# A windowed attention with channel mixing on one core: two-token rows, halves of v moved by DMA, x transposed by the crossbar

## The chip, the cores and the metric

The kernel runs on one core of a Trainium2 chip. The metric is the device time in microseconds of one execution, as the median of several runs. A core has five engines with their own instruction streams: TensorE (PE; its weight loads are listed as PEld), VectorE (DVE), ScalarE (ACT), GpSimd (POOL) and SyncE (SP), which here issues nearly all the transfers. The engines wait for each other by semaphores.

## What is computed

Inputs are q, k and v of shape [4, 8, 768, 64] (4 sequences, 8 heads, 768 tokens, 64 wide), all float32. Attention is causal with a window of 128 tokens, and the first four tokens (the sinks) are seen by every query:

```python
scores = q @ k.T / sqrt(64)
keep = (pos_k < 4) | ((pos_q - pos_k >= 0) & (pos_q - pos_k < 128))
a = softmax(where(keep, scores, -1e9))
x = (a @ v)                        # heads side by side: [4, 768, 512]

x_prev = x shifted by one token, 0 ahead of the first
xk = mu_k * x + (1 - mu_k) * x_prev
xr = mu_r * x + (1 - mu_r) * x_prev
k = relu(xk @ w_k)                 # [.., 1024]
v = (k * k) @ w_v                  # [.., 512]
out = sigmoid(xr @ w_r) * v
```

(The reference writes the first `k` and `v` of the second half with names of their own; they have nothing to do with the attention's.)

## The kernel before

The kernel works in 12 blocks of 256 tokens, u = 0 to 11, three for each sequence: b is the sequence and T = 0, 1, 2 the block in it. Every operation is registered with an engine, and a list for each engine (ORDER) gives the order of the operations by number; another (CHOICE) gives the engine of those that could run on more than one. Buffers come from pools and are handed out in that order.

A block goes through four steps. `prepare` casts k and q to bf16 and transposes them, so that the head dimension lies on partitions, with TensorE and an evacuation, or with a transposing DMA through the crossbar (k from block 4 on, q from block 8 on). Where TensorE transposes, k and q come with two neighbouring tokens in one row (`j` is the parity), and the evacuation undoes that by a strided write. v comes with one token in a row and 256 B in a run:

```python
# load
if name == "v":
    for g in range(2):
        s0 = 256 * T + 128 * g
        ... nc.sync.dma_start(out=buf[key][:, g, :, :],
                              in_=v[b, :, s0:s0 + 128, :].rearrange("h p d -> p h d"))
...
# otherwise, two tokens in a row
        ... nc.sync.dma_start(out=buf[key][:, h0:h1, :, :].rearrange("p h j d -> p h (j d)"),
                in_=src[b, h0:h1, 256 * T:256 * T + 256, :].rearrange(
                    "h (p j) d -> p h (j d)", j=2))
...
# prepare: evacuation of transposed k and q
out=buf[key][:, 2 * half:2 * half + 2, :, :].rearrange("p c g (t j) -> p c j (g t)", j=2),
in_=buf[psk].bitcast(BF16)[:, 0:512].rearrange("p (c j t) -> p c j t", c=2, j=2)
```

`attend` works by pairs of heads (c = 0 to 3). Scores of two pairs are made in one go, the exponential follows on ScalarE, VectorE multiplies it by a mask of ones and zeros, and TensorE multiplies by v. A column of ones beside v gives the sum of the weights; VectorE divides. In a first block (T = 0) no earlier keys exist and the scores are 768 wide for a pair instead of 1024. For later blocks the sinks are scored apart (`es`, `vsink`).

```python
jobs = [(kt[:, c, 0, :], 128, 384, qt[:, c, :, :]), (kt[:, c, 1, :], 384, 512, qt[:, c, 1, :])]
if T > 0:
    jobs.append((buf["kt", u - 1][:, c, 1, :], 0, 128, qt[:, c, 0, :]))
for (lhs, o0, o1, rhs) in jobs:
    for a in range(2):
        rows = slice(64 * a, 64 * a + 64)
        nc.tensor.matmul(out=sc[:, a, o0:o1], lhsT=lhs[rows], rhs=rhs[rows], ...)
...
nc.scalar.activation(out=buf[ek][:, :, lo:], in_=buf[sck][:, :, lo:], func=AF.Exp, scale=scale)
...
nc.vector.tensor_tensor(out=at, in0=at, in1=m, op=ALU.mult)      # the mask
...
# values: for each half g of the queries, the sinks, then two key blocks for each head
```

`mix` transposes x with TensorE, copies it from PSUM into `xt` (a sequence's tokens side by side, with a zero ahead), and blends neighbouring tokens:

```python
P.op("PE", 225.0, transpose, ...)            # 4 transposes for each half of the channels
P.op("ACT", act(512), evacuate(...), ...)    # or VectorE; two for each block
...
nc.vector.tensor_tensor(out=buf[tk], in0=xt[:, c0:c0 + 2, t0:t0 + 256],
                        in1=xt[:, c0:c0 + 2, t0 - 1:t0 + 255], op=ALU.subtract)
# then for xk and xr, and for each of four channel groups
nc.vector.scalar_tensor_tensor(out=buf[key][:, c0 + i, :], in0=buf[tk][:, i, :],
    scalar=mu[w][:, c0 + i:c0 + i + 1], in1=xt[:, c0 + i, t0 - 1:t0 + 255],
    op0=ALU.mult, op1=ALU.add)
```

`ffn` then makes keys (32 matmuls of 256 columns), relu, square, the gate (8 matmuls of 512, a tanh in place of the sigmoid) and the product with w_v (16 matmuls of 512), and stores 128 tokens at a time. The step of block u-1 is interleaved with the attention of block u. While TensorE has nothing to do early on, it multiplies a tile `warm` by itself.

Of the kernel before, what the change touches and what calls it, by code (L numbers as in the profile page):

```python
# [16 lines left out]

CHOICE = {
    78: "ACT", 81: "ACT", 82: "ACT", 84: "ACT", 86: "ACT", 88: "DVE", 93: "DVE", 94: "DVE", 96:
    "DVE", 100: "DVE", 101: "DVE", 127: "DVE", 133: "DVE", 135: "DVE", 136: "DVE", 139: "ACT",  # L20
    140: "DVE", 149: "DVE", 190: "DVE", 191: "ACT", 192: "ACT", 217: "DVE", 264: "DVE", 272:
    "DVE", 277: "DVE", 304: "DVE", 342: "DVE", 345: "DVE", 347: "DVE", 351: "ACT", 353: "DVE",
    360: "DVE", 422: "DVE", 428: "ACT", 429: "ACT", 498: "DVE", 500: "DVE", 503: "DVE", 506:
    "DVE", 507: "ACT", 519: "DVE", 585: "ACT", 586: "ACT", 653: "DVE", 657: "DVE", 659: "DVE",
    662: "DVE", 671: "DVE", 735: "DVE", 737: "ACT", 738: "DVE", 743: "DVE", 750: "DVE", 814:
    "DVE", 815: "ACT", 824: "DVE", 884: "DVE", 886: "DVE", 890: "ACT", 891: "ACT", 1002: "DVE",
# [3 lines left out]
QD = range(8, 12)  # L30

XD = ()

BEGIN = {"SP": 800.0, "PE": 1260.0, "ACT": 2600.0, "DVE": 930.0, "POOL": 930.0}

TOGETHER = 2

RING = 2600
# [10 lines left out]
        89, 92, 105, 95, 98, 103, 116, 108, 113, 131, 137, 141, 128, 124, 119, 155, 134, 157,  # L49
        148, 183, 189, 168, 235, 207, 208, 211, 212, 219, 220, 160, 165, 171, 176, 215, 193,  # L50
        180, 200, 216, 186, 237, 290, 298, 291, 294, 299, 302, 248, 303, 225, 295, 240, 245,
        306, 223, 227, 276, 231, 228, 251, 260, 232, 266, 256, 310, 263, 283, 269, 311, 318,
        343, 308, 314, 329, 315, 348, 366, 374, 367, 375, 321, 370, 394, 326, 371, 332, 337,
        396, 274, 352, 378, 359, 379, 382, 407, 384, 386, 421, 387, 444, 452, 445, 453, 399,
        426, 404, 474, 410, 415, 390, 430, 391, 456, 437, 457, 448, 472, 485, 449, 462, 525,
        529, 526, 530, 499, 537, 460, 504, 538, 468, 509, 469, 553, 477, 482, 533, 493, 488,
        534, 511, 564, 556, 464, 578, 465, 541, 518, 543, 561, 549, 583, 572, 550, 587, 545,
        567, 631, 601, 546, 602, 605, 613, 606, 594, 629, 642, 614, 619, 609, 617, 610, 639,
        634, 677, 681, 678, 682, 663, 645, 689, 705, 707, 685, 650, 686, 690, 625, 670, 718,
        710, 621, 626, 693, 622, 760, 756, 764, 757, 761, 765, 721, 695, 740, 726, 715, 774,  # L60
        784, 701, 749, 768, 742, 769, 795, 702, 787, 792, 697, 772, 698, 816, 776, 780, 777,
        781, 834, 830, 838, 831, 835, 798, 839, 858, 860, 842, 803, 846, 843, 823, 854, 848,
        868, 863, 871, 855, 906, 914, 907, 850, 915, 851, 879, 874, 910, 892, 911, 918, 899,
        919, 934, 936, 922, 924, 930, 947, 931, 972, 939, 973, 980, 944, 981, 950, 976, 958,
        977, 955, 984, 926, 965, 985, 927, 990, 988, 1000, 1008, 1004, 1001, 1012, 1005, 1013,
        1009, 992, 1020, 996, 993, 997, 1016, 1018, 1021, 1028, 1024, 1029, 1025,
    ),
    "DVE": (
        70, 71, 88, 93, 94, 100, 96, 107, 101, 112, 109, 114, 110, 136, 104, 115, 118, 127, 123,
        143, 125, 120, 133, 121, 126, 135, 149, 144, 150, 151, 145, 152, 190, 146, 159, 147,  # L70
        164, 79, 80, 153, 69, 170, 140, 175, 161, 162, 166, 172, 167, 177, 173, 178, 154, 195,
        196, 202, 197, 204, 203, 210, 217, 198, 222, 205, 206, 83, 239, 244, 304, 199, 85, 241,
        305, 242, 246, 214, 247, 255, 218, 87, 277, 250, 293, 297, 278, 229, 252, 301, 253, 233,
        257, 258, 279, 264, 342, 285, 347, 280, 281, 286, 288, 345, 320, 287, 312, 325, 316,
        272, 336, 289, 322, 331, 323, 327, 282, 328, 333, 338, 334, 339, 369, 353, 275, 373,
        354, 360, 357, 361, 381, 355, 377, 363, 356, 362, 422, 388, 398, 403, 409, 400, 414,
        405, 401, 365, 411, 416, 406, 417, 412, 358, 364, 447, 432, 392, 433, 439, 434, 441,
        440, 455, 459, 498, 481, 476, 503, 451, 528, 500, 487, 506, 435, 492, 510, 436, 470,
        478, 479, 483, 443, 484, 494, 555, 495, 489, 540, 490, 442, 536, 557, 571, 513, 558,
        560, 532, 466, 514, 519, 562, 520, 563, 516, 566, 573, 521, 574, 515, 522, 589, 551,  # L80
        568, 590, 569, 517, 524, 547, 523, 653, 633, 592, 638, 596, 659, 598, 657, 591, 597,
        604, 644, 635, 640, 636, 641, 649, 599, 616, 600, 612, 665, 646, 593, 608, 647, 651,
        709, 652, 668, 662, 666, 692, 667, 711, 671, 672, 674, 673, 675, 712, 627, 680, 623,
        669, 735, 720, 714, 725, 722, 723, 676, 684, 727, 728, 688, 759, 716, 741, 717, 763,
        791, 786, 750, 767, 738, 743, 788, 789, 793, 744, 703, 794, 745, 771, 751, 747, 802,
        746, 753, 752, 754, 699, 818, 778, 782, 797, 819, 748, 821, 833, 799, 755, 800, 837,
        804, 805, 814, 862, 841, 867, 824, 825, 820, 845, 826, 864, 827, 865, 869, 884, 856,
        822, 878, 886, 870, 828, 873, 852, 875, 880, 881, 876, 909, 829, 917, 894, 897, 913,
        901, 895, 921, 902, 938, 903, 943, 896, 932, 949, 940, 941, 945, 946, 951, 954, 952,
        904, 956, 957, 898, 960, 961, 905, 967, 975, 962, 969, 968, 928, 979, 963, 971, 987,  # L90
        983, 1002, 964, 1003, 1007, 970, 1011, 1015, 994, 998, 1022, 1030, 1026,
    ),
    "ACT": (
        91, 90, 97, 111, 106, 99, 68, 67, 117, 130, 122, 132, 142, 138, 129, 182, 188, 163, 158,
        184, 78, 156, 174, 169, 81, 139, 209, 221, 236, 213, 179, 185, 194, 201, 181, 191, 187,
        243, 238, 292, 82, 300, 192, 254, 226, 249, 84, 296, 307, 86, 224, 259, 265, 261, 262,
        268, 267, 284, 270, 340, 324, 319, 344, 309, 335, 330, 349, 368, 376, 395, 372, 418,
        402, 397, 380, 420, 383, 423, 408, 385, 413, 351, 425, 446, 454, 427, 480, 475, 431,
        496, 438, 428, 501, 458, 450, 473, 486, 463, 527, 531, 429, 491, 461, 505, 539, 559,
        554, 507, 577, 535, 512, 570, 575, 579, 580, 582, 542, 544, 565, 584, 585, 588, 637,  # L100
        632, 603, 586, 655, 595, 607, 615, 630, 620, 643, 618, 611, 648, 679, 683, 664, 706,
        708, 713, 687, 691, 731, 729, 719, 733, 694, 724, 737, 758, 766, 762, 696, 775, 790,
        785, 770, 808, 796, 806, 801, 773, 812, 810, 817, 832, 836, 840, 859, 861, 866, 844,
        847, 815, 882, 849, 877, 872, 888, 908, 916, 893, 912, 900, 935, 920, 937, 942, 890,
        923, 891, 925, 948, 974, 953, 982, 959, 966, 986, 978, 991, 989, 1006, 1014, 1010, 1019,
        1017,
    ),
    "POOL": (
        73, 72, 74, 75, 76, 102, 77, 273, 271, 350, 508, 661, 739,
    ),  # L110
    "SP": (
        0, 1, 2, 3, 4, 5, 7, 6, 16, 8, 9, 10, 11, 15, 17, 12, 18, 13, 14, 19, 20, 25, 23, 24,
        21, 234, 22, 341, 346, 28, 30, 29, 313, 26, 27, 419, 424, 31, 230, 33, 34, 35, 32, 497,
        36, 317, 502, 37, 40, 38, 389, 39, 45, 393, 41, 576, 581, 42, 467, 43, 44, 46, 47, 654,
        656, 660, 658, 548, 48, 51, 49, 50, 471, 53, 52, 732, 730, 734, 736, 54, 628, 57, 58,
        55, 552, 56, 624, 809, 807, 704, 813, 811, 59, 60, 61, 779, 63, 64, 62, 700, 883, 885,
        889, 887, 65, 857, 66, 853, 933, 929, 783, 995, 999, 1023, 1031, 1027,
    ),
}


class Plan:

# [8 lines left out]
    def pool(self, name, tiles):  # L137
        self.pools[name] = list(tiles)

    def op(self, engine, cost, emit, rank, reads=(), writes=(), take=(), hold=(), port=False,  # L140
           lag=None, service=0.0, descs=128, mode=0, alts=None):
        i = len(self.ops)
        if i in CHOICE:
            engine = CHOICE[i]
# [5 lines left out]
    def schedule(self):  # L150
# [42 lines left out]
        while any(lines.values()):  # L193
# [32 lines left out]
            if o["port"]:  # L226
                port[o["engine"]] = t + o["cost"]
# [53 lines left out]
def kernel(  # L281
# [36 lines left out]
    for name in ("ks", "qs", "vs"):  # L318
        pool(name, 3, [128, 2, H, D] if name == "vs" else [128, H, 2, D], FP32)
# [640 lines left out]
```

The softmax here doesn't subtract the row's maximum and nothing guards it: scores larger than these inputs give would overflow.

## Time and profile before

| | before |
|---|---|
| median of 3 runs | 171.7 us (170.59 to 172.16) |
| span of the profiled execution | 169.6 us |
| VectorE instructions, GpSimd instructions | 403, 31 |
| transfers: mean rate, packets | 199 GB/s, 82803 |
| HBM read, written | 24.12 MB, 6.29 MB |
| transposes through the crossbar | 16 of k, 8 of q; median 2.5 and 2.4 us from issue to landing |
| loads of v | 24 of 256 KB; median 4.6 us to landing |

The profile page gives for each engine the time in which an instruction was in work. Instructions of an engine overlap at their ends, so that the mean duration of one in a group is more than the distance from its start to the next start. Where the pace matters it is read from the list of instructions in order of time, whose columns are start, duration, engine, line of the kernel, operation and operands; consecutive ones of a kind are merged and counted (x12). In the slices, each of 40 figures stands for 4.24 us, in tenths. A group line ends with the idle time of the engine just before its instructions and with what ended most of it.

### The profile page before, as it was taken

What the parts mean: (1) busy time and instruction counts of PE and PEld (TensorE: products, weight loads), DVE (VectorE), ACT (ScalarE), POOL (GpSimd) and SP (SyncE); (2) the same over time, 40 slices, a digit from 0 to 9 for tenths busy, and PEclk for the clock granted to TensorE, in tenths of its full rate; (3) what the DMA queues carried; (4) which work ended last, traced back from release to release, by engine and by line L of the source; (5) the groups of instructions that cost most, each with busy time, mean ns of one, the idle gap of its engine ahead of it and who ended that gap; (6) DMA issues with size and microseconds to landing.
All of it is one profiled execution on the core that took longest, in us unless ns stands there. A gap on an engine that the chain in (4) does not pass through costs nothing.

```text
span 169.6 us, 4184 instructions
## 1 busy us (share of the span) xinstructions
PE 160.0 (94%) x1602; PEld 105.7 (62%) x1602; DVE 153.4 (90%) x403; ACT 129.0 (76%) x208; POOL 13.5 (8%) x31
## 2 busy tenths in 40 slices
PE   7977879799999999999999999999999999999992
PEld 2544658664657667767567786756476775877551
DVE  6288898999999999999999999999999999799542
ACT  3588797999898999897979986866829849953320
POOL 6330000000200010050000200030000000000000
PEclk9995699999999999999999999999999999999999
DMA  5999989999938979999579489969969858103033
GB/s 142 238 275 320 344 192 326 356 335 276 191 86 214 254 172 231 184 263 287 135 183 221 97 207 225 181 168 233 252 147 266 195 109 233 62 4 124 2 124 124
DMA packets 82803, 33.82 MB, mean 199 GB/s; under 512 B 64736, under 2 KB 77280, under 8 KB 82784
## 3 DMA queue, kind: packets, MB, share of 16 engines
q1 hardware_dynamic: 81728, 33.56, 80.0%
q8 instruction: 12, 0.20, 0.5%
q10 hardware_dynamic: 1056, 0.00, 0.4%
q14 instruction: 7, 0.06, 0.1%
HBM read 24.12 MB, written 6.29 MB: 179 GB/s over the span
## 4 chain that ended last, share of the span: by engine, by line
PE 82%; DVE 10%; DMA 3%; SPq 1%; issue 1%; ACT 0%; POOL 0%; DVEq 0%
PE bank L888 24%; PE bank L839 23%; PE bank L870 12%; PE bank L713 7%; PE sc L654 6%; DMA vs<-in_v_dram 3%; PE bank L752 3%; PE bank L569 2%; PE bank L701 2%; DVE e L690 2%; DVE xk L789 2%; SPq L387 1%; DVE x L729 1%; PE bank L631 1%; PE bank L809 1%
## 5 line engine op out<-in xcount | busy, mean ns | idle before, releaser
L839 PE MATMUL bank<-xk,wk_sb 128*128 128x256 bf16 x384 | 50.5, 273 | 1.1 <-DVE wk_sb L513 0.9
L676 ACT ACTIVATE e<-sc 128x1024 bf16<-128x1024 f32 (+1 forms) x48 | 44.6, 966 | 4.4 <-PE sc L654 4.4
L888 PE MATMUL bank<-wv_h,kk 128*128 128x512 bf16 x184 | 45.8, 379 | 0.0
L839 PEld LDWEIGHTS <-wk_sb 128*128 128x128 bf16 x384 | 35.3, 98 | 9.3 <-DVE wk_sb L513 1.4
L849 ACT ACTIVATE rl<-bank 128x512 bf16<-128x512 f32 x45 | 26.2, 607 | 10.3 <-PE bank L839 7.8
L690 DVE TENSOR_TENSOR e<-e,mask 128x1024 bf16<-128x1024 bf16 (+1 forms) x48 | 30.1, 639 | 0.4 <-POOL ksink L608 0.3
L888 PEld LDWEIGHTS <-kk 128*128 128x128 bf16 x184 | 16.7, 98 | 15.7 <-issue 0.5
L870 PE MATMUL bank<-wr_sb,xr 128*128 128x512 bf16 x96 | 24.2, 379 | 0.0
L789 DVE SCALAR_TENSOR_TENSOR xk<-td,mu,xt 128x256 bf16<-128x256 bf16 x48 | 22.4, 493 | 0.1
L789 DVE SCALAR_TENSOR_TENSOR xr<-td,mu,xt 128x256 bf16<-128x256 bf16 x48 | 22.5, 477 | 0.0
L876 ACT ACTIVATE th<-bank 128x512 f32<-128x512 f32 x24 | 14.8, 620 | 7.8 <-PE bank L870 7.7
L729 DVE TENSOR_TENSOR x<-bank,rec 128x256 bf16<-128x256 f32 x48 | 19.4, 416 | 0.6 <-DVE rec L726 0.3
L897 DVE SCALAR_TENSOR_TENSOR ob<-th,bank 128x512 f32<-128x512 f32 x23 | 15.6, 681 | 4.7 <-ACT th L876 2.6
L861 DVE TENSOR_TENSOR kk<-rl 128x512 bf16<-128x512 bf16 x48 | 19.4, 416 | 0.1
L713 PE MATMUL bank<-vb,e 128*128 128x65 bf16 x352 | 19.2, 195 | 0.2
L713 PEld LDWEIGHTS <-e 128*128 128x128 bf16 x352 | 16.7, 99 | 3.1 <-issue 0.6
L654 PE MATMUL sc<-qt,kt 64*128 64x128 bf16 (+1 forms) x256 | 14.8, 247 | 1.1 <-ACT kt L577 0.7
L870 PEld LDWEIGHTS <-xr 128*128 128x128 bf16 x96 | 8.9, 98 | 8.6 <-issue 0.3
L654 PEld LDWEIGHTS <-kt 64*128 64x128 bf16 x256 | 9.5, 97 | 7.3 <-issue 4.0
L761 ACT COPY xt<-bank 128x512 bf16<-128x512 bf16 x15 | 8.8, 587 | 5.3 <-PE bank L752 4.5
L701 PE MATMUL bank<-vsink,es 128*128 128x130 bf16 x64 | 12.4, 220 | 0.3 <-ACT rl L849 0.3
L779 DVE TENSOR_TENSOR td<-xt 128x512 bf16<-128x512 bf16 x24 | 10.5, 440 | 0.1
(63 smaller groups left out, 163.9 us busy)
## 6 DMA issues: line engine op xcount, KB each, us to landing
vs<-in_v_dram SPq DMA_DIRECT2D x24, 256.0 KB, 4.6
out_dram<-ob SPq DMA_DIRECT2D x23, 256.0 KB, 3.3
ks<-in_k_dram SPq DMA_DIRECT2D x18, 256.0 KB, 4.8
qs<-in_q_dram SPq DMA_DIRECT2D x7, 512.0 KB, 7.3
qs<-in_q_dram SPq DMA_DIRECT2D x10, 256.0 KB, 5.3
w<-in_moe_w_k_dram SPq DMA_DIRECT2D x2, 1024.0 KB, 10.3
w<-in_moe_w_v_dram SPq DMA_DIRECT2D x2, 1024.0 KB, 10.0
ks<-in_k_dram SPq DMA_DIRECT2D x3, 512.0 KB, 8.2
```

Of the source, the lines that this page charges most:

```text
L654: nc.tensor.matmul(out=sc[:, a, o0:o1], lhsT=lhs[rows], rhs=rhs[rows], start=True, stop=True)
L676: nc.scalar.activation(out=buf[ek][:, :, lo:], in_=buf[sck][:, :, lo:], func=AF.Exp, scale=scale)
L690: nc.vector.tensor_tensor(out=at, in0=at, in1=m, op=ALU.mult)
L701: nc.tensor.matmul(out=o[:, g, :, :], lhsT=buf["es", u][:, 128 * g:128 * g + 128], rhs=vsink[b % 2][:, 2 * c:2 * c + 2, :], start=True, st ...
L713: nc.tensor.matmul(out=o[:, g, a, :], lhsT=e[:, a, e0:e0 + 128], rhs=rhs, start=(T == 0 and i == 0), stop=(i == len(blocks) - 1), skip_gro ...
L729: P.op("DVE", dve(256), lambda ok=ok, rk=rk, c=c: nc.vector.tensor_tensor(out=buf["x", u][:, :, 128 * c:128 * c + 128].rearrange("p g (a d ...
L789: nc.vector.scalar_tensor_tensor(out=buf[key][:, c0 + i, :], in0=buf[tk][:, i, :], scalar=mu[w][:, c0 + i:c0 + i + 1], in1=xt[:, c0 + i, t ...
L839: nc.tensor.matmul(out=ps[:, i, :], lhsT=wk_sb[:, c, 128 * f:128 * f + 128], rhs=xk[:, c, :], start=(c == 0), stop=(c == NC - 1), skip_gro ...
L849: nc.scalar.activation(out=buf[rk], in_=buf[psk].rearrange("p (i t) -> p i t", i=2), func=AF.Relu)
L861: P.op("DVE", dve(512, 0.52), lambda f2=f2, rk=rk: nc.vector.tensor_tensor(out=buf["kk", u][:, 2 * f2:2 * f2 + 2, :], in0=buf[rk], in1=buf ...
L870: nc.tensor.matmul(out=buf[psk], lhsT=buf["xr", u][:, c, 128 * g:128 * g + 128], rhs=wr_sb[:, c, :], start=(c == 0), stop=(c == NC - 1))
L888: nc.tensor.matmul(out=buf[psk], rhs=wv_h[:, f, :], lhsT=buf["kk", u][:, f, 128 * g:128 * g + 128], start=(f == 0), stop=(f == NF - 1))
```

## The change

The arrangement of tokens changes. All of q, k and v now come with two neighbouring tokens in a row (512 B in a run), and the parities are kept apart from there on: a block of 256 queries is two groups of 64 pairs of tokens, ordered odd before even, keys of a whole sequence lie in one tile, even before odd, and stores take every second row of the output. So the strided evacuation of k and q goes, and with it the one-token loads of v, k and q.

- A group's window then begins in the middle of a block's rows. The value matmul of the first group needs half of the rows of the block before and half of its own in one tile `vj`; these halves are moved by DMA within the chip for blocks from 3 on, and by a copy on VectorE or ScalarE before that.
- In the first blocks of sequences 2 to 4 (u = 3, 6, 9) the first 64 pairs see only themselves; both parities of their 64 keys are stacked over the 128 partitions, so that one matmul does for two.
- Blocks 0 and 1 get no mask on VectorE: TensorE writes a bias (0 or -30000) into the scores' PSUM first, by a matmul with the identity, and the scores are added.
- x of blocks 6 to 11 is transposed by the crossbar and not by TensorE.
- The fused blend (difference times mu plus neighbour) becomes three kinds of step: a difference of 512 elements, a scaling by mu (on VectorE or ScalarE), and an addition of 512 elements. An edge copy, on GpSimd or VectorE, puts the last token of a group beside the first of the next.
- mu comes as rows and is transposed on TensorE. GpSimd may take casts of k, q and a weight. CHOICE, ORDER and the constants that the lists were made with are new throughout, and the early loads come in halves by heads, with two blocks of q, k and v ahead of w_k.

```diff
+BIAS = (0,1)
+XD = range(6,12)
+VJD = range(3, 12)
+STACK = (3, 6, 9)
...
-            if name == "v":
-                for g in range(2):
-                    ... in_=v[b, :, s0:s0 + 128, :].rearrange("h p d -> p h d")
+            key, src = (name, u), {"k": k, "q": q, "v": v}[name]
+            ... in_=src[b, h0:h1, 256 * T:256 * T + 256, :].rearrange("h (p j) d -> p h (j d)", j=2)
...
-                    out=buf[key][:, 2 * half:2 * half + 2, :, :].rearrange(
-                        "p c g (t j) -> p c j (g t)", j=2),
+                    out=buf[key][:, 2 * half:2 * half + 2, :, :],
...
+            for g, w in ((1, u - 1), (0, u)):
+                if u in VJD:
+                    P.op("SP", 400.0, lambda g=g, w=w: nc.sync.dma_start(
+                        out=buf[vj][64 - 64 * g:128 - 64 * g].rearrange("p j h d -> p (j h d)"),
+                        in_=buf["vb", w][64 * g:64 * g + 64].rearrange("p j h d -> p (j h d)")), rank,
...
+            for j in range(2):
+                for g in range(2):
+                    at = 128 * T + 64 * (g - 1) * (T > 0)
+                    for a in range(2):
+                        rows = slice(64 * a, 64 * a + 64)
+                        nc.tensor.matmul(
+                            out=sc[:, a, :].rearrange("p (j g t) -> p j g t", j=2, g=2)[:, j, g],
+                            lhsT=kt[rows, c, j, at:at + 128], rhs=q2[rows, g],
+                            start=u not in BIAS, stop=True, skip_group_check=u in BIAS)
+        def biased(cs):
+            for c in cs:
+                for a in range(2):
+                    nc.tensor.matmul(out=buf["sc", u, c][:, a, :], lhsT=ident, start=True,
+                                     rhs=bias[T].to_broadcast([128, 2, 2, 128]), stop=False,
+                                     skip_group_check=True)
...
+            else:
+                P.op("SP", 1200.0, lambda g=half: nc.sync.dma_start_transpose(
+                    out=xt[:, :, at + g, 16:144], in_=buf["x", u][:, g, :]),
...
+            return lambda: copy(out=xt[:, :, at + 1:at + 1 + n, 15:16],
+                                in_=xt[:, :, at:at + n, 79:80])
...
-            P.op("DVE", dve(512, 0.5), lambda c0=c0, tk=tk: nc.vector.tensor_tensor(
-                out=buf[tk], in0=xt[:, c0:c0 + 2, t0:t0 + 256],
-                in1=xt[:, c0:c0 + 2, t0 - 1:t0 + 255], op=ALU.subtract), ...
-                        nc.vector.scalar_tensor_tensor(
-                            out=buf[key][:, c0 + i, :], in0=buf[tk][:, i, :],
-                            scalar=mu[w][:, c0 + i:c0 + i + 1],
-                            in1=xt[:, c0 + i, t0 - 1:t0 + 255], op0=ALU.mult, op1=ALU.add)
+            P.op("DVE", dve(512, 0.52), lambda g=g: nc.vector.tensor_tensor(
+                out=block(xr, g), in1=behind(g), op=ALU.subtract, ...
+                    nc.vector.tensor_scalar(
+                        out=buf[key][:, c, :], in0=buf[xr][:, c, :],
+                        scalar1=mu[w][:, c:c + 1], scalar2=None, op0=ALU.mult)
+                    # or, on ScalarE
+                    nc.scalar.activation(out=buf[key][:, c, :], in_=buf[xr][:, c, :],
+                                         func=AF.Copy, scale=mu[w][:, c:c + 1])
+                    nc.vector.tensor_tensor(out=part, in0=part, in1=behind(g), op=ALU.add)
...
-                nc.sync.dma_start(out=out[b, s0:s0 + 128, :], in_=buf[bk])
+                nc.sync.dma_start(out=out[b, s0 + 1 - g:s0 + 256:2, :], in_=buf[bk])
```

The lists ORDER and CHOICE, the building of masks and sinks, and the model's constants are cut here.

## The prediction

> **What bounds the kernel now.** I read the spans and clocks first (one core, 169.6 us in the profile, clock 0.98), then the busy shares and the slices, then windows of 5 us, then TensorE in order of time, and last the costliest groups and the DMA part. From the page:
>
> ```profile
> PE 160.0 (94%) x1602; PEld 105.7 (62%) x1602; DVE 153.4 (90%) x403; ACT 129.0 (76%) x208; POOL 13.5 (8%) x31
> ...
> PE   7977879799999999999999999999999999999992
> ...
> DVE  6288898999999999999999999999999999799542
> ...
>
> ```
>
> TensorE is full from about slice 9 on, and so nearly is VectorE. Before that both have holes, and the clock falls to half. The windows say it more exactly (columns: stretch, its length, then busy time and instructions of TensorE, weight loads, VectorE, ScalarE, GpSimd, the clock, the DMA share and GB/s):
>
> ```profile
> 10.00:15.00 5.00, 3.29 (x41) 2.06 (x41) 4.68 (x13) 4.02 (x7) 1.34 (x3) 0.83 1.11 264
> 15.00:20.00 5.00, 4.64 (x53) 3.28 (x52) 3.73 (x12) 3.92 (x7) 0.00 (x0) 0.50 1.05 378
> 20.00:25.00 5.00, 3.24 (x29) 2.16 (x26) 5.00 (x12) 5.00 (x8) 0.00 (x0) 0.98 0.89 199
> ...
> 30.00:35.00 5.00, 4.12 (x50) 3.21 (x50) 5.00 (x13) 5.00 (x8) 0.00 (x0) 1.00 1.05 367
> 35.00:40.00 5.00, 5.00 (x44) 2.97 (x43) 5.00 (x14) 5.00 (x9) 0.00 (x0) 1.00 1.16 310
> ```
>
> A busy TensorE need not be at its peak, so I take its pace from starts in order of time:
>
> ```profile
> 154.11 3.66 PE L839 MATMUL bank<-xk,wk_sb 128*128 128x256 bf16 x32
> 157.60 4.48 PE L888 MATMUL bank<-wv_h,kk 128*128 128x512 bf16 x20
> 161.92 1.89 PE L870 MATMUL bank<-wr_sb,xr 128*128 128x512 bf16 x8
> ```
>
> Start to start, 32 matmuls of 256 columns take 3.49 us (0.109 each) and 20 of 512 take 4.32 us (0.216). In the same way I read 0.55 us for two head pairs of scores with a window behind them (12 matmuls), 0.44 without (8), 0.18 for one sink matmul and its four value matmuls, 0.53 for the 12 value matmuls of a first block, 0.22 for four transposes, 0.23 for the sink scores. The whole kernel without its warming matmuls is then 280 x 0.216 + 4 x 0.216 + 400 x 0.109 + 64 x 0.18 + 8 x 0.53 + 16 x 0.55 + 8 x 0.44 + 48 x 0.22 + 8 x 0.23 = 145.4 us. By 35.3 us it has done 15.9 us of that (56 key matmuls 6.1, 16 transpose groups 3.5, scores 3.1, values 2.5, the rest 0.7). So 19.4 us are lost before 35.3. From there to its last matmul at 166.4 it has 129.5 us of work in 131.1: it loses 1.6. Then 3.2 us of last product and store. So two things are worth time: the loss at the start, and work taken off TensorE.
>
> **What the skill says.** (1) "TensorE: Matmul & The Clock Gate", under "What's actually happening": an array that idles through a window of some 3.4 us falls to half clock. The trace agrees in kind: 3.29 of 5 us busy at 10 to 15, then a clock of 0.50 at 15 to 20. (2) "VectorE: DVE Perf Modes", the perf-mode tier table: bf16 tensor_tensor reaches 2x, a bf16 tensor_scalar 4x. The groups below agree for tensor_tensor: twice the elements of the fused form in less time. No row shows the 4x. (3) "DMA: Bandwidth & Descriptors", Specifications: line rate wants 512 B or more; here most packets are below. (4) "VectorE: DVE Perf Modes", "The three transpose paths": the crossbar is slower than TensorE for one 128x128 block. Here a crossbar transpose of keys lands 2.5 us after its issue, and four blocks on TensorE take 0.22 and an evacuation.
>
> ```profile
> L789 DVE SCALAR_TENSOR_TENSOR xr<-td,mu,xt 128x256 bf16<-128x256 bf16 x48 | 22.5, 477 | 0.0
> L789 DVE SCALAR_TENSOR_TENSOR xk<-td,mu,xt 128x256 bf16<-128x256 bf16 x48 | 22.4, 493 | 0.1
> L690 DVE TENSOR_TENSOR e<-e,mask 128x1024 bf16<-128x1024 bf16 x32 | 21.3, 681 | 0.2 <-ACT e L676 0.2
> L779 DVE TENSOR_TENSOR td<-xt 128x512 bf16<-128x512 bf16 x24 | 10.5, 440 | 0.1
> ```
>
> ```profile
> DMA packets 82803, 33.82 MB, mean 199 GB/s; under 512 B 64736, under 2 KB 77280, under 8 KB 82784
> ```
>
> The means of VectorE hold some 90 ns of overlap with the next one; start to start I read 0.395 us for the fused form, 0.335 for the difference, 0.60 for the wide mask and 0.465 for the narrow one.
>
> **The change, part by part.** Counts of after are from its instruction streams.
>
> *TensorE, steady.* x of blocks 6 to 11 goes by the crossbar: 12 groups of four transposes less, -2.6 us. Three stacked first blocks now take 16 score matmuls per two head pairs: 6 x (0.55 - 0.44) = +0.7. Sink rows need two matmuls: +0.7 with the three later sequences. Sum -1.3 us, on the bound. *TensorE, start.* 16 matmuls of 512 columns add the mask as a bias in blocks 0 and 1 (+3.5 us), block 0 has eight more value matmuls and more score columns, and its sink rows a second matmul (+0.6), and 16 warming matmuls stand for 22. This falls into a stage with 19.4 us of loss.
>
> *VectorE.* 96 fused (37.9 us) and 24 differences (8.0) go. In come 72 tensor_tensor of 512 (24.1) and 50 tensor_scalar of 256, an estimate of 0.13 each from the skill's formula in "VectorE: DVE Perf Modes" ((58 + 64) cycles at 0.96 GHz), 6.5. Masks: 28 wide and 12 narrow for 32 and 16, -4.3. Three fewer x evacuations -1.0, 13 q/k evacuations at 0.335 for 7 at 0.63, 0; five more relus +3.0, two copies of v +0.9 (estimate), a cast more, a weight cast less. Sum about -16 of 145: VectorE stops being a second bound.
>
> *ScalarE.* 46 scalings come, 0.3 each by the pitch of the 256-column exponential: +13.8. Against that 11 fewer casts (-5.5), nine fewer x evacuations (-4.5), 17 strided q/k evacuations of 0.61 become 11 of 0.5 (-5), five relus fewer (-2.5), two copies of v (+1.9, estimate), exponentials about +0.9. Sum -1: unchanged.
>
> *DMA.* v, and the later k and q, come in 512 B runs: 49152 packets of 256 B become 24576. Twelve more crossbar transposes and 18 moves inside the chip take much of it back. At the start only the gain counts.
>
> *Where the start ends now.* ScalarE's stream in order, from the first q at 4.6 us: 6 casts or v copies of 0.51, 4 evacuations of 0.5, 6 exponentials of 0.93, a v move of 0.97, sink exponential and scaling of 0.3 each, two more casts and two exponentials: 14.1 us, so 18.7 without a wait. I allow 1.8 for waits: block 1's values end near 20.5. The weights allow the same: 5.5 MB are asked for up to the second half of w_k, and before moves 5.6 MB by 21 us. TensorE has then done 8.1 us of real work (11 transpose groups, four score groups, values of two blocks, sinks). ScalarE then has 18.0 us up to the fourth exponential of block 2, TensorE 15.7. So at 38.5 us, 23.8 us are done. Before it has 15.9 + 3.2 - 0.3 = 18.8 by 38.5. The lead is 5.0 us. What is left is 145.4 - 1.3 + 0.6 (start extras without the bias) - 23.8 = 120.9, plus the old 1.6 of small waits and 3.2 at the end: 38.5 + 120.9 + 1.6 + 3.2 = 164.2 us in a profile, 5.4 under 169.6. The median stands 2.1 above its profile, so **166.3 us**.
>
> **Rivals.** (A) *The start is bound by the transfers.* For it: DMA shares of 1.05 to 1.14 between 5 and 20 us; q, k, v of two blocks now come ahead of w_k. Then only the 1.3 us and a little of the v packets remain: about 169. Against: TensorE waited 0.9 us only for a cast of w_k, and ScalarE and VectorE read 5.00 of 5 at 20 to 25. (B) *New waits.* The new path from x to xk has a crossbar transpose (2.5 us against some 1.1 for transpose and evacuation), a small edge copy on GpSimd whose like (ksink) took 0.19 to 2.4 us, and six mixing steps in a chain. If each of six late blocks costs TensorE 0.5 to 1 us, 3 to 6 come back: 169 to 172. Against: in the last block there are 9 us of other TensorE work between its values and its keys, and the chain needs about 7.3 (x 0.43, two transposes 4.5, edge 0.3, mixing 2.1). (C) *The start gets dense,* the clock does not fall, and VectorE's freedom takes the 1.6 too: 161 to 163.
>
> **Range and chances.** The centre takes the ScalarE pace; A and B pull up by 3 to 5, C down by 4. I think C or the centre likelier than A or B together. 161.3 to 170.7 should hold 8 times in 10. Over 2% faster means below 168.3, which is 2 above the centre: 0.70. Within 2%: 0.24. Slower than 175.1 needs B in every block: 0.06.
>
> **What would show it.** Right: the clock no longer reads 0.50 for a whole window at 15 to 20; key matmuls of block 0 start near 21 but with block 1's values done; L789's 45 us gone, tensor_scalar near 0.13 to 0.2; VectorE under 85% busy; TensorE still without waits after 40 us; some 43000 fewer packets under 512 B (49152 and 1056 of mu less, about 600 more for each of twelve transposes). Wrong: TensorE waits with xt, xk or edge copies as releasers after 80 us (B), waits for weights or casts until 25 us (A), or GpSimd casts, which took 0.75 to 1.17 us before, holding up keys.

## The result, and the profile after

The changed kernel takes 188.95 us (188.19 to 192.28) against 171.63 us (170.59 to 172.16) before: 1.1008 times the time, with a 95% interval of 1.0959 to 1.1058. Its profile has a span of 187.4 us where before has 169.6. I had predicted 166.3 us. The page of the changed kernel, engines, slices and packets:

```profile
PE 165.1 (88%) x1705; PEld 105.2 (56%) x1705; DVE 143.3 (76%) x411; ACT 133.0 (71%) x224; POOL 25.8 (14%) x73
...
PE   7998799999998989997969299997899299999992
...
PEclk9999999999999999999999889999999969999999
...
DMA packets 64885, 37.42 MB, mean 200 GB/s; under 512 B 21080, under 2 KB 58592, under 8 KB 64864
```

VectorE is less busy, as meant, the clock stays up at the start, as meant, and TensorE, which had no hole after 40 us, has many, down to 2 tenths of a slice. The table of windows gives their sum. The columns are stretch, length, TensorE's busy time with its records, granted clock, DMA share and GB/s; first the kernel before, then the changed one:

```profile
40.00:160.00 120.00, 119.89 (x1245) 1.00 0.79 179
```

```profile
40.00:160.00 120.00, 105.10 (x1142) 0.97 0.86 190
```

In 120 us TensorE stands still for 14.9 us, where it stood for 0.1. The waits of TensorE in the changed kernel (the time, how often, the longest):

```profile
PE bank L1019 <- DVE rl L1033: 3.7, 1, 3.7
PE bank L1019 <- DVE xk L973: 3.5, 1, 3.5
PE bank L1068 <- DVE x L870: 1.8, 1, 1.8
...
PE bank L1050 <- DVE xr L973: 1.1, 1, 1.1
```

L1019 is the key matmuls, L1050 the gate's, L973 the addition of the neighbour's column. The second of these waits, followed in time. The order of time on SyncE's queue, VectorE and TensorE around 100 us, all of the changed kernel:

```profile
92.61 3.29 SPq L914 DMA_TRANSPOSE xt<-x  x2
...
101.96 5.84 SPq L914 DMA_TRANSPOSE xt<-x  x2
```

```profile
101.85 0.28 DVE L953 TENSOR_SCALAR xk<-xr,mu_all 128x256 bf16<-128x256 bf16 x1
105.81 0.77 DVE L973 TENSOR_TENSOR xk<-xk,xt 128x512 bf16<-128x512 bf16 x2 [3.69 <-ACT xr L958]
```

```profile
102.10 1.03 PE L1068 MATMUL bank<-wv_h,kk 128*128 128x512 bf16 x4
106.63 1.01 PE L1019 MATMUL bank<-xk,wk_sb 128*128 128x256 bf16 x4 [3.50 <-DVE xk L973]
```

The transposes at 92.61 are block 6's; both halves are in and both differences made by 100.5. The addition at 105.81 is block 6's too, and its scalings are done at 102.1. The trace puts its wait down to ScalarE, whose scaling of xr ends at 105.67; but what is added to here is xk. The first transpose of the pair issued at 101.96 lands at 105.69, 0.12 us before the addition, and that pair is block 7's. A wait for several semaphores shows only one name. The built program says the same. Its instruction streams, with the semaphores that matter here:

```
DVE  L973 TensorTensor xk2_110<-xk2_110,xt0_150   [waits DMAHW7, DVE, Activation]   block 6
SP   L914 DmaTranspose xt0_150<-x1_106            [counts on DMAHW7]                block 7, first
SP   L914 DmaTranspose xt0_150<-x1_106            [waits DMAHW0, DVE]               block 7, second
```

Blocks 6, 7 and 8 are one sequence and share one tile, xt0_150, in different columns. The neighbours are read by an access pattern built by hand, which starts at the second parity's columns and steps back by 65 to the first's; before, they were read as plain slices of the tile. So block 6's addition waits for block 7's first transpose, which writes columns that it never reads. The wait goes the other way too: the count of DVE that the second transpose waits for is that of block 6's addition. SyncE, which issues in order, stands from 103.22 us until the addition ends at 106.58:

```profile
106.61 1.19 SPq L914 DMA_TRANSPOSE xt<-x  x1
```

Waits of additions for the next block's transposes stand in the streams for blocks 7 (at 129 us) and 9 (at 148 us) as well. The waits of 3.7 and 1.1 us above follow from them: behind block 9's late addition VectorE comes late to the relu that frees a bank, and block 7's gate needs its late addition. That is theory F, the false wait. Its rivals: L, the crossbar's own latency; M, late transfers of v ahead of 90 us, where TensorE had already lost ground without any x on the crossbar.

### The profile page after: what moved, and what is told of

Its sections match the earlier page's. It is cut to its first block, busy times and chain, and to the rows that moved or that the text cites. A ratio compares the mean times of both kernels' runs of the same rounds, so it can differ in the third digit from the quotient of the medians.

```text
span 187.4 us, 4514 instructions
## 1 busy us (share of the span) xinstructions
PE 165.1 (88%) x1705; PEld 105.2 (56%) x1705; DVE 143.3 (76%) x411; ACT 133.0 (71%) x224; POOL 25.8 (14%) x73
## 4 chain that ended last, share of the span: by engine, by line
PE 56%; DVE 18%; DMA 15%; SPq 5%; issue 2%; ACT 1%; DVEq 0%; ACTq 0%
PE bank L1019 18%; PE bank L1068 17%; DMA xt<-x 10%; PE bank L1050 6%; SPq L404 4%; DVE x L870 4%; PE bank L848 3%; DMA vs<-in_v_dram 3%; DVE e L823 3%; DMA vj<-vb 2%; PE sc L778 2%; DVE xr L943 2%; PE sc L763 1%; PE bank L640 1%; PE bank L842 1%
## 5 line engine op out<-in xcount | busy, mean ns | idle before, releaser
L1019 PE MATMUL bank<-xk,wk_sb 128*128 128x256 bf16 x384 | 50.5, 280 | 7.8 <-DVE rl L1033 3.7
L1019 PEld LDWEIGHTS <-wk_sb 128*128 128x128 bf16 x384 | 36.8, 100 | 17.0 <-issue 9.0
L1029 ACT ACTIVATE rl<-bank 128x512 bf16<-128x512 f32 x40 | 22.7, 602 | 22.1 <-PE bank L1019 22.1
L823 DVE TENSOR_TENSOR e<-e,mask 128x1024 bf16<-128x1024 bf16 (+1 forms) x40 | 25.6, 652 | 0.5 <-ACT e L813 0.5
L1050 PE MATMUL bank<-wr_sb,xr 128*128 128x512 bf16 x96 | 24.0, 379 | 1.1 <-DVE xr L973 1.1
L973 DVE TENSOR_TENSOR xk<-xk,xt 128x512 bf16<-128x512 bf16 x24 | 9.6, 419 | 8.7 <-DMA xt<-x 4.8
L958 ACT ACTIVATE xr<-xr,mu_all 128x256 bf16<-128x256 bf16 x26 | 13.0, 506 | 2.4 <-DVE xk L953 2.3
L867 DVE RECIPROCAL rec<-bank 128x4 f32<-128x4 f32 x48 | 8.3, 176 | 8.2 <-PE bank L848 8.0
L848 PE MATMUL bank<-vb,e 128*128 128x65 bf16 x208 | 14.0, 193 | 0.5 <-ACT e L813 0.3
L1050 PEld LDWEIGHTS <-xr 128*128 128x128 bf16 x96 | 8.7, 98 | 9.7 <-DVE xr L973 1.8
L973 DVE TENSOR_TENSOR xr<-xr,xt 128x512 bf16<-128x512 bf16 x24 | 9.7, 418 | 4.9 <-DMA xt<-x 3.7
L778 PE MATMUL sc<-qt,kt 64*128 64x128 bf16 x288 | 11.4, 217 | 0.6 <-DMA kt<-kb 0.4
L943 DVE TENSOR_TENSOR xr<-xt 128x512 bf16<-128x512 bf16 x24 | 9.9, 423 | 2.4 <-DMA xt<-x 1.8
```

The source lines that it names most:

```text
L778: nc.tensor.matmul(out=sc[:, a, :].rearrange("p (j g t) -> p j g t", j=2, g=2)[:, j, g], lhsT=kt[rows, c, j, at:at + 128], rhs=q2[rows, g] ...
L823: nc.vector.tensor_tensor(out=part, in0=part, op=ALU.mult, in1=m.unsqueeze(1).to_broadcast([128, 2, width // 2]))
L848: nc.tensor.matmul(out=o[:, g, a, :], lhsT=buf[ek][:, a, 128 * j:128 * j + 128] if u in STACK else e[:, a, j, g, :], rhs=vv[:, j, 2 * c + ...
L973: nc.vector.tensor_tensor(out=part, in0=part, in1=behind(g), op=ALU.add)
L1019: nc.tensor.matmul(out=ps[:, i, :], lhsT=wk_sb[:, c, 128 * f:128 * f + 128], rhs=xk[:, c, :], start=(c == 0), stop=(c == NC - 1), skip_gro ...
L1029: nc.scalar.activation(out=buf[rk], in_=buf[psk].rearrange("p (i t) -> p i t", i=2), func=AF.Relu)
```

## The experiments: the false wait and the crossbar

**e1_tiles.** The tile is split, nothing else.

```diff
-    xts = [tile1([128, NC, 2 * NT, STEP], BF16, f"xt{i}") for i in range(2)]
+    xts = [[tile1([128, NC, 2, STEP], BF16, f"xt{i}_{T}") for T in range(NT)] for i in range(2)]
-        xt, at = xts[b % 2], 2 * T
+        xt, at = xts[b % 2][T], 0        # and two edge copies instead of one
```

> The changed kernel (189.0 us) with one edit: the transposed x has a tile of its own for each block instead of one tile for a sequence, so the additions of the neighbour's columns in one block share no tile with the crossbar transposes of the next block; the engines' orders stay, and GpSimd's edge copy becomes two copies. Theory F (the additions were released by the next block's crossbar transposes): the three late releases near 106, 129 and 148 us go, the stretches 100 to 110 and 145 to 150 us fill, and the time falls by 8 to 12 us, to 177 to 181 us. Rival L (the crossbar's own latency sets the loss): at most 2 us less, 187 us or more. Rival M (the loss is made before 90 us, by late v and key transfers): at most 3 us less, 186 us or more.

Measured: 179.59 us, 9.4 less; 1.0479 times before (1.0444 to 1.0515). The addition's wait for a transfer is gone from the stream, and so is the second transpose's wait for the addition. In the trace the addition follows its scaling at once, and the pair of transposes holds SyncE's stream for 2.51 us where it was 5.84 (VectorE, TensorE, SyncE of this kernel):

```profile
101.18 0.28 DVE L956 TENSOR_SCALAR xk<-xr,mu_all 128x256 bf16<-128x256 bf16 x1
101.56 0.77 DVE L976 TENSOR_TENSOR xk<-xk,xt 128x512 bf16<-128x512 bf16 x2
```

```profile
102.39 0.60 PE L1022 MATMUL bank<-xk,wk_sb 128*128 128x256 bf16 x4
```

```profile
101.29 2.51 SPq L915 DMA_TRANSPOSE xt<-x  x2
```

The keys start at 102.39 instead of 106.63. F holds, in mechanism and size. A part of it is the clock: in the changed kernel it falls after both long waits, to 0.8 and 0.6 in the slices above, and in e1 it is 1.00 over 40 to 160 us. It is not the backward step that makes other columns count as read: built with a forward step over the same elements, the program has the same waits, and built with two plain slices of the shared tile in place of the pattern it has none of them, in either direction. So it is the pattern built by hand. Neither of these two was timed.

**e2_x_pe and e4_tiles_x_pe.** x of the last six blocks goes by TensorE again, in the shared tile (e2) and in split tiles (e4).

```diff
-XD = range(6,12)
+XD = ()          # 12 groups of transposes and 12 evacuations put into the engines' orders
```

> The changed kernel with x of the last six blocks transposed on TensorE again (24 groups of four become part of its line, half of them evacuated by ScalarE and half by VectorE), in the sequence-wide tile as it is; nothing is on the crossbar but keys and queries. Both F and L take the loss of the last six blocks to come with the crossbar's x and expect about 177 to 181 us (the transposes give back 2.6 us of TensorE work). Rival M expects 185 us or more, since its loss lies before 90 us, where no x goes through the crossbar.

> Both edits, a tile for each block and x of the last six blocks on TensorE. Theory F: about as the kernel with tiles alone plus up to 2 us of TensorE work (178 to 182 us), as the crossbar costs nothing once nothing waits on the next block's. Rival L: 3 us or more below the kernel with tiles alone, since the crossbar's latency is still in that one.

Measured: 178.39 (1.0406, 1.0373 to 1.0438) and 179.00 us (1.0445, 1.0383 to 1.0507). With x off the crossbar, the split brings nothing more, and with split tiles leaving the crossbar brings 0.6. F's numbers, and L seemed to fall. It fell too soon: TensorE's way adds 12 x 0.22 = 2.6 us of its own work and 12 evacuations, so with a gain of 0.6 the crossbar itself costs some 3 us, an estimate that takes the evacuations as free (k2 below).

**e3_vj_dve.** In the changed kernel as it is, the moves of v for blocks with earlier queries are copied by VectorE.

```diff
-VJD = range(3, 12)
+VJD = ()
```

> The changed kernel with the halves of v of blocks with earlier queries copied by VectorE (12 copies of about 0.42 us, 5 us of VectorE work) instead of by DMA; stacking and crossbar stay. Rival M (late v transfers make the loss of 6 us between 40 and 90 us): 3 to 6 us less, 183 to 186 us. Theories F and L: within 2 us of 189, as the waits at 100 to 110 and 145 to 150 us stay.

Measured: 187.45 us, 1.5 less. Below M's 3 to 6, and within the 2 us of F and L. But here the false waits stand behind every gain.

## The experiments: the other 8 us

Split tiles leave 8 us over the kernel before, and 13 over the prediction.

**e5_no_moves, e6_vj_pool, e7_no_stack.** e5 is e4 with `VJD = ()`. e6 is e1 with the moves of v on another queue. e7 is e1 with `STACK = ()` and the wide mask of a first block.

```diff
-                P.op("SP", 400.0, lambda j=j: nc.sync.dma_start(      # e6
+                P.op("POOL", 400.0, lambda j=j: nc.gpsimd.dma_start(
```

> A tile of its own for each block, x of the last six blocks on TensorE, and also the halves of v of blocks with earlier queries copied by VectorE (5 us more of it): of the added transfers only the six small ones for the stacked blocks are left. If the added transfers and their issues on the one in-order queue make the rest of the loss (theory Q), this is 3 us or more below the kernel with tiles and x on TensorE (179.0): 173 to 176 us. If the loss lies in the engines' orders or in the stacked scores (rival O), it stays at 178 to 181 us.

> The kernel with a tile for each block (179.6 us, crossbar x kept), with the 18 moves of v issued from GpSimd's queue instead of the queue of all loads, stores and crossbar transposes. Theory Q (the one in-order queue delays loads and transposes behind moves that wait for their casts): 2 to 5 us less, 175 to 178 us. Rival O (orders or stacked scores) and a rival that the moves' own latency counts: within 1.5 us of 179.6.

> The kernel with a tile for each block, with the first blocks of the later three sequences unstacked: 16 score matmuls and 12 value matmuls per two head pairs on 1024 columns instead of 16 and 8 or so on 768, masks and exponentials wide, and the six small moves of v gone. By the pitches, 3 blocks get about 6 x (0.88 - 0.79) us of scores and 12 x 0.13 of values more on TensorE, 12 x 0.14 us more masks on VectorE and 12 x 0.3 us more exponentials. If stacking is a gain as meant: 1 to 4 us slower, 181 to 184 us. If the wait for the stacked moves (1.2 us before the values of block 6) and the halved score matmuls cost more than they save: 178 to 179 us.

Measured: e5 180.55 us (1.0509, 1.0436 to 1.0582), e6 177.12 (1.0320, 1.0221 to 1.0419), e7 179.83 (1.0488, 1.0402 to 1.0573). e6 is 2.5 under e1: the moves cost something by standing in SyncE's queue. e5 does not confirm it: there 12 copies of 0.42 us stand in VectorE's stream instead, and whether they give back what the moves cost is not shown. e7 equals e1: stacking and its six moves together are neither gain nor loss. The chain of e1 shows why its gain is small, with two pairs of stacked scores (two groups of full and two of half height each):

```profile
73.24 0.22 PE sc L764 x4
73.64 0.22 PE sc L764 x4
74.04 0.97 PE bank L1071 x4
```

From 73.24 to 74.04 are 0.8 us for two pairs, where I had estimated 0.55.

**e8_reorder and e9_before_reorder.** e6 and, as the control, the kernel before, both with new values of `ORDER` and `CHOICE` from the same search.

> The kernel with a tile for each block and the moves of v on GpSimd's queue (177.1 us), with the same operations in a new order on each engine and some evacuations and casts on another engine, found by a search that minimises the planned end with costs taken from the traces (stacked scores 0.79 us for two head pairs, scores with a window 0.55, the edge copies 0.43, GpSimd's casts 0.72 to 0.88, transfers up to 1 us later than planned). Rival O (what is left of the loss is in orders that were fitted to other costs): 3 to 6 us less, 171 to 174 us. If the rest is contention that no order avoids (theory Q alone): 176 to 178 us.

> The kernel before (171.6 us), with nothing but its operations in a new order, found by the same search with the same kind of costs: the control for the run beside it. If the old order was already fitted to the chip: 170 to 173 us, no gain. If any order gains by this search: 168 to 170 us, and then the change itself is to be judged by the two reordered kernels against each other.

Measured: 179.59 us (1.0467, 1.0406 to 1.0527) and 178.34 us (1.0363, 1.0291 to 1.0434). The control is the answer: an order that looks better on paper costs the kernel before 7 us. So e8 says nothing of O, the rival by which the loss lies in the engines' orders.

**e10_stores_pool and e11_before_stores.** 23 stores go from SyncE's queue to GpSimd's, in e6 and in the kernel before.

```diff
-            P.op("SP", 400.0, store, rank, ...)      # nc.sync.dma_start
+            P.op("POOL", 400.0, store, rank, ...)    # nc.gpsimd.dma_start
```

> The kernel with a tile for each block and the moves of v on GpSimd's queue (177.1 us), with 23 of the 25 output stores on GpSimd's queue as well, so that SyncE's queue, whose issues stand nearly end to end from 44 to 140 us, holds only loads and crossbar transposes. Theory Q (what is left is made by the one in-order queue): 2 to 4 us less, 173 to 175 us, with loads issued earlier. Rival O (what is left lies in the engines' orders): within 1.5 us of 177.1.

> The kernel before (171.6 us) with the same 23 stores on GpSimd's queue, as the control. Before has 74 transfers on its queue from 44 us on against the changed kernel's 100 or so, and TensorE has next to no waits there: within 1 us of 171.6 by both theories; 1 us or more slower if a store from GpSimd's queue costs something of itself.

Measured: e10 182.20 us (1.0614, 1.0540 to 1.0688), 5.1 worse than e6, and e11 173.56 us (1.0125, 1.0050 to 1.0201), 1.9 over its own before: stores on GpSimd's queue cost something there too. Q, by which the one in-order queue makes the rest, falls as I had put it, and the waits of e10 say why. GpSimd's stream stops at stores that are not ready, the moves of v stand behind them, and TensorE waits for the moves, 5.6 us against 1.4 in e6 (the first line is GpSimd's, the others TensorE's):

```profile
POOL out_dram L1078 <- DVE ob L1071: 36.1, 8, 9.0
```

```profile
PE bank L840 <- DMA vj<-vb: 3.9, 2, 2.5
...
PE bank L828 <- DMA vj<-vb: 1.7, 2, 1.3
```

So the question became how much each added transfer costs, in whatever queue.

**k1 to k4.** Each is e6 with transfers left out and everything else as it is; the plan keeps their places in the orders.

```diff
-                   lambda g=g, w=w: nc.gpsimd.dma_start(          # k1, k3, k4: no moves of v
+                   lambda g=g, w=w: OUT or nc.gpsimd.dma_start(   # OUT = True
-                    vv = buf["vb" if g or T == 0 else "vj", u]
+                    vv = buf["vb" if g or T == 0 or u > 2 else "vj", u]
-                lambda g=half: nc.sync.dma_start_transpose(        # k2, k3, k4: no crossbar x
+                lambda g=half: OUT or nc.sync.dma_start_transpose(
-       lambda key=key, src=src: nc.sync.dma_start(                 # k4: no loads from block 5 on
+       lambda key=key, src=src: (u > 4 and OUT) or nc.sync.dma_start(
```

> The kernel with a tile for each block and the moves of v on GpSimd's queue (177.1 us), with the 18 moves of v left out: the values matmuls read the block's own v in their place, so the output is not the reference's, and matmuls, engines' orders and all else stay. From 38.5 us on that kernel has 123.1 us of TensorE work by the pitches, 3.2 of tail and 10.1 lost, against 2.7 lost in the kernel before. If the moves' latency makes a part of it (theory V): 2 to 4 us less, 173 to 175 us. Rivals X (crossbar x), T (late loads) and O (orders of the engines): within 1 us.

> The same kernel (177.1 us) with the 12 crossbar transposes of x left out: the mixing reads what earlier blocks left in the tiles, so the output is not the reference's. Theory X (their latency, or their place in the queue, still costs): 2 to 4 us less, 173 to 175 us. V, T and O: within 1 us.

> Both left out. V and X together: 171 to 174 us, about the sum of the two gains. O or T: 175 us or more.

> Both left out and also the loads of k, q and v of the last seven blocks, whose casts then read what earlier blocks left: nothing after about 60 us waits for a load, a move of v or a transpose of x, only for crossbar transposes of keys and queries. If transfers of any kind make the rest of the loss (V, X or T): 168 to 170 us, the dense 167 plus what the kernel before loses too. If the orders of the compute engines make it (O): within 1 us of the run with both left out.

Measured: k1 172.76 us (1.0093, 1.0060 to 1.0126), k2 172.78 (1.0145, 1.0074 to 1.0216), k3 169.46 (0.9933, 0.9903 to 0.9962), k4 169.41 (0.9889, 0.9869 to 0.9909). By the medians the moves are worth 4.4 us under e6, the crossbar 4.3, both 7.7, the loads nothing. e6 was not run again beside them, and its interval is 2% wide: by the ratios to the kernel before, the moves are worth 3.9 us, the crossbar 3.0, both 6.6. The windows of e1, e6, k3 and k4, in this order; e1's trace lacks 16 matmuls of 512 columns in this stretch, so its busy time is low by up to 16 x 0.22 = 3.5 us:

```profile
40.00:160.00 120.00, 111.30 (x1201) 1.00 0.88 197
```

```profile
40.00:160.00 120.00, 115.41 (x1248) 1.00 0.91 200
```

```profile
40.00:160.00 120.00, 119.53 (x1277) 1.00 0.71 172
```

```profile
40.00:160.00 120.00, 119.94 (x1282) 1.00 0.31 80
```

TensorE is as dense in k3 as it was before, with the orders unchanged. So V (the moves of v) and X (the crossbar's x) hold. T, the late loads, falls: in k4 the DMA share drops from 0.71 to 0.31 and the time stays. O falls as far as the orders alone would make the loss; whether another order would hide the added transfers stays open. Nor do these runs part a transfer's latency from its place in a queue.

**e12_vj_load, e13_vj_load_x_pe, e14_vj_copy.** Versions that compute the reference, all from e1: v fetched a second time from HBM, cast on the way (e12), that with x on TensorE (e13), and the moves as copies by GpSimd (e14).

```diff
-   P.op("SP", 400.0, lambda g=g, w=w: nc.sync.dma_start(out=buf[vj][...], in_=buf["vb", w][...]))
+   nc.gpsimd.dma_start(out=buf[vj][..., 0:D], in_=v[b, :, t0 + j:t0 + 128:2, :])          # e12, e13
+   P.op("POOL", 1200.0, lambda g=g, w=w: nc.gpsimd.tensor_copy(out=buf[vj][...], ...))    # e14
```

> A version to keep: the kernel with a tile for each block, in which the halves of v are not moved from the cast v but fetched from HBM a second time by GpSimd's queue, cast on the way, some 3 us earlier in that queue since they wait for no cast. V and X explain the rest: the 4.3 us of the moves' latency goes, the crossbar's 4.3 stays: 172 to 174 us, about as without the moves (172.8). If the fetches with their 64 x 8 runs of 256 B are slow to issue or crowd the loads: 175 us or more.

> The same with x of the last six blocks on TensorE: without moves and crossbar 169.5, plus 24 groups... that is 12 groups of four transposes at 0.22 us, 2.7 us, plus small waits on 12 evacuations: 171.5 to 174 us. It would beat the kernel before (171.5) only if the evacuations cost nothing.

> The kernel with a tile for each block (179.6 us, crossbar x kept), with the 18 moves of v made by GpSimd itself as copies of 64 partitions instead of by DMA: no transfer latency, about 1.1 us a copy as ScalarE's took, on an engine that is 16% busy. If the moves' latency is what counts (V) and the copies disturb nothing: 174 to 176 us. If GpSimd's copies hold up VectorE or its own casts: 178 us or more.

Measured: e12 187.19 us (1.0940, 1.0839 to 1.1041); e13 a median of 189.26 (185.66 to 190.50), without a ratio, since three of its four executions fell into the core's slower state, at a lower clock; e14 176.39 (1.0360, 1.0242 to 1.0477). The fetches seem to crowd the transfers. In e12's DMA part one takes 6.3 us, and the DMA share over 40 to 160 us is 1.36, where e1 has 0.88 (TensorE's busy time is low here too, as 15 records are missing):

```profile
vj<-in_v_dram POOLq DMA_DIRECT2D x30, 64.0 KB, 6.3
```

```profile
40.00:160.00 120.00, 105.78 (x1142) 0.97 1.36 191
```

e14 is 3.2 under e1, just above the range I gave for V, and less than the 6.8 by which k1 is under it; what holds the rest is not shown. It is 4.8 over the kernel before. No version that computes the reference beats the kernel before. Only k3 and k4 are under it, and they leave work out.

## Why the prediction was wrong, step by step

The whole difference of 22.7 us between 166.3 and 188.95 has four parts, in the order of the runs: 9.4 false wait (e1), 2.5 place in SyncE's queue (e6), 7.7 added transfers beyond that (k3; 6.6 by the ratios), and 3.2 from k3's 169.46 to the prediction. The last is 2.5 of work left at 38.5 us (123.4, not 120.9) and 1.3 of small waits (2.9, not 1.6), less 0.6 because k3's median stands 1.5 above its profile, not 2.1. A time over 175.1 us had been given a chance of 0.06.

**The start: right in kind, short in size.** The clock no longer falls: 1.00 in all windows up to 100 us. But the lead is smaller. Priced by the prediction's pitches, with the stacked scores at their measured 0.79, before has done 19.3 us of work at 38.5 us (predicted 18.8; I had counted 56 key matmuls by 35.3 us, and there are 60), and the changed kernel 22.8 without the bias, where 23.8 were predicted. The lead is 3.5, not 5.0. The step that failed is "block 1's values end near 20.5", paced by ScalarE: they end at 23.1. The times that I listed for ScalarE come to 15.1 us, not 14.1. And the last values wait for VectorE, to which I had given no part in the start; its mixing of block 0 stands ahead of the normalisation that frees a bank (TensorE, then VectorE, of the changed kernel):

```profile
22.59 0.22 PE L842 MATMUL bank<-vsink,es 128*128 128x130 bf16 x1 [0.84 <-DVE x L870]
```

```profile
19.73 1.25 DVE L953 TENSOR_SCALAR xk<-xr,mu_all 128x256 bf16<-128x256 bf16 x2
20.91 0.41 DVE L649 COPY kt<-bank 128x512 bf16<-128x512 bf16 x1
21.24 0.75 DVE L973 TENSOR_TENSOR xk<-xk,xt 128x512 bf16<-128x512 bf16 x2
```

**TensorE's steady work: -1.3 predicted; the sum failed by one term.** Stacked scores cost 0.79 for two pairs, not 0.55: 6 x 0.24 = 1.4 us more. Without the bias's 3.5 us the changed kernel holds 146.3 us and before 145.4: 0.9 more, where I had 0.7 less (-1.3 and the start's 0.6). Nothing is taken off the bound. So the most this change can bring is 3.5 - 0.9 = 2.6 us, where I had 5.0 + 0.7 = 5.7.

**"The old 1.6 of small waits": the step that cost most.** With the bias the changed kernel holds 149.8 us of work. At 38.5 us it has 123.6 of it left and then 3.2 of tail, in 148.9: 22.1 are lost. By the same prices before loses 1.8, and k3 loses 168.0 - 38.5 - 123.4 - 3.2 = 2.9. (k1's expectation has 123.1, 10.1 and 2.7 for what e6 has left, what it loses and what before loses; by these pitches they are 123.9, 9.3 and 1.8.) Rival B named the path from x to xk and asked for 0.5 to 1 us a block. k2 shows 4.3 in six blocks (3.0 by the ratios), which is its size. I argued B away with the last block, 9 us of other work against a chain of 7.3, as if each block waited for its own transposes alone. What B lacked was the wait on the next block's, worth 9.4; it stood in the instruction streams, where I had counted instructions and not read waits.

**The moves of v: no step at all.** I counted their packets ("take much of it back") and gave them no latency, though they lie between a block's cast and its values. They are worth 4.4 us by k1 (3.9 by the ratios), and 2.5 more by standing in SyncE's queue. The transfers in the changed kernel (median us to landing in the last column), and then the same row before for the keys' transposes:

```profile
vj<-vb SPq DMA_DIRECT2D x12, 130.0 KB, 4.0
...
kt<-kb SPq DMA_TRANSPOSE x16, 4.5
...
xt<-x SPq DMA_TRANSPOSE x12, 2.7
```

```profile
kt<-kb SPq DMA_TRANSPOSE x16, 2.5
```

**VectorE and ScalarE: right in direction, without effect.** L789's 45 us are gone and VectorE is 76% busy. The groups of the new mixing in the changed kernel:

```profile
L953 DVE TENSOR_SCALAR xk<-xr,mu_all 128x256 bf16<-128x256 bf16 x28 | 8.4, 318 | 0.1
L953 DVE TENSOR_SCALAR xr<-xr,mu_all 128x256 bf16<-128x256 bf16 x22 | 6.3, 295 | 0.0
```

```profile
L958 ACT ACTIVATE xr<-xr,mu_all 128x256 bf16<-128x256 bf16 x26 | 13.0, 506 | 2.4 <-DVE xk L953 2.3
```

Start to start a scaling takes 0.20 us on VectorE, not 0.13, and 0.41 on ScalarE, not 0.3. The Trainium skill, "VectorE: DVE Perf Modes", section "The TRN2 errata", had the better term: it says that the fixed part measures some 150 cycles rather than 58, so (150 + 64) at 0.96 GHz is an estimate of 0.22. VectorE's busy time fell by 10 instead of 16 us and ScalarE's rose by 4 instead of falling by 1. With the added transfers out TensorE is dense in k3, so neither was the bound after the start, and the misjudged sums of both are not a part of the 22.7 there.

**Packets: right.** 43656 fewer under 512 B, against "some 43000". k4 shows that, with the added transfers out, fewer bytes bring nothing after the start.

## What to carry to other kernels

When a new operation reads a shared tile with an unusual pattern (here one built by hand instead of a slice), list which writes its instructions wait for before believing any time. A transfer put between two engines is priced by its landing and by the in-order queue that issues it, in every block, not by its packets; leaving it out in a run shows that price in one number. An order of instructions that was never run on the chip can itself be a cost: on the kernel before, the one that was tried looked better and cost 7 us.

## What was not expected of the hardware

The transposes of keys landed 2.5 us after issue before and 4.5 after the change (medians), with 12 transposes and 18 moves more in the queue. A move of 130 KB inside the chip took 4.0 us to land. In fetches with runs of 256 B and a cast, 64 KB took 6.3 us, and the DMA share rose to 1.36. Moving 18 small transfers to GpSimd's queue gained 2.5 us, and moving 23 stores there as well lost 5.1: which queue is free counts less than what stands ahead of the urgent transfer in it.
